# Copies of q and k that write in sequence, pooled scores and local values in other PSUM tiles, and a new order of instructions

## The chip, the cores and the metric
One core of a Trainium2 chip runs the whole kernel in one launch. The metric is device time in microseconds (us). Five engines work on their own instruction lists, each in its list's order: TensorE (PE in the profile, PEld its weight loads), VectorE (DVE), ScalarE (ACT), GpSimd (POOL) and SyncE (SP). SP and ACT also issue the DMAs.

## The reference
Everything is fp32. 2304 tokens (4 batches of 576) pass through an attention and two products with gates:

```python
# attention: per batch and head, S = 576, D = 64, factor 4; scale = 1 / sqrt(D)
q_d, k_d, v_d = means of q, k, v over 4 tokens each
out_up    = repeat(softmax(scale * q_d @ k_d.T) @ v_d, 4)
out_local = softmax(where(|i - j| < 4, scale * q @ k.T, -1e9)) @ v
x = (out_up + out_local)                 # as (2304, 512)
# first layer: d_ff = 2048
h = x @ w_in;  x = (h * sigmoid(1.702 * h)) @ w_out
# second layer: d_ff = 1024
out = ((x @ w1) * (x @ w2) @ w3) @ w_out2
```

## The kernel before
**Products.** Each fp32 product is made of three (`mm3`, lines 305 to 307): both operands are split into a high and a low part by `split` (a copy on ScalarE, line 301, and a subtraction, line 302, mostly on VectorE), and the four 128-row pieces of the inner dimension add up in one PSUM bank. The weights come in as 64-bit numbers, read as pairs of 32-bit words; ScalarE (line 353) and three operations on VectorE (lines 360 to 366) make fp32 of them.

**Stages.** From the start to about 110 us TensorE makes the product of w3 and w_out2 (`w34_transpose`, `w34_mm`), and the attention of batch 0 is woven in between. Then come the first layer's five blocks of up to 512 tokens: for each of 16 slices f of the hidden width an `h_step` (4 x 3 products into a bank, gelu `g_t` on ScalarE at line 810, split) and, two slices later, a `y_step` (into four banks y0 to y3). The attention of batches 1 to 3 is woven into these until about 405 us. Then the second layer runs, with seven half-size products in the place of eight (`ab_step`), to the end.

**Attention.** The heads go in 16 pairs, n = 4 b + hp, two heads on the 128 partitions. Of a pair, `t_piece` transposes q and k on TensorE (line 471, four transpositions into one tile) and ScalarE copies the tile out (line 472): in PSUM the elements stand as (r, u), with r the place within a group of four tokens and u the group; in SBUF as (u, r). That is so in batches 0 and 1, 4 copies a pair, 32 in all; in batches 2 and 3 VectorE transposes. `s_local` makes local scores in two halves (line 515), bounds them by the mask (518) and takes the maximum (519). `s_pool` makes the pooled scores (`ps_sp`, products on line 534) and their maximum (536). In batches 0, 2 and 3 the exponentials read the pooled scores out of PSUM piece by piece (`s_exp`, line 495, `own_exp` True); in batch 1 VectorE subtracts the maximum first and one exponential follows. `p_piece` transposes the weights of the softmax (577) and copies them out (578). `v_pool` makes pooled values (`ps_vp`, products on line 592) and copies them out with a factor (`od`, line 595). `v_local` makes local values in two halves (line 604, 10 and 8 products), adds the pooled ones (608, reads the PSUM tile and `od`) and stores the sum to x_d (612). In the four pairs of `LOCAL` (12 to 15) the local part is not on TensorE but on VectorE and GpSimd, and only pooled scores and values go through PSUM.

**PSUM.** There are eight banks: y0 to y3 (pool `psy`, one tile each; products of w3 and w_out2, then second products of the first layer), two of tag "h" (pool `psh`: first products of the first layer and transposed w3, line 759) and two of tag "t" (pool `pst`: all PSUM tiles of attention). A tile of a tag gets its bank when the tile before the last of that tag has been read by all that read it.

**What sets the order.** `ORDER` (lines 20 to 185) has for each engine a list of positions in the program's own sequence ("12+7" are 12 to 19), and `ACROSS` (186 to 205) pairs of positions on two engines, such as "2:18<4:21". At the end of the program both are put in as dependences without a semaphore, so the scheduler must keep that order. Weights, windows of v (`att_load_v`) and all stores go out on SP, most loads of q, k and v on ACT until batch 2; POOL makes the masks (`setup`). Other tags touched: "ys", "g" and "xr" in SBUF (pool `g2p`, two tiles each); "ys" holds the local results `xo`, the products `w34s` and others, "xr" the tiles of x loaded for the first layer, "g" gelu's output.

Of the kernel before, what the change touches and what calls it, by code (L numbers as in the profile page):

```python
# [8 lines left out]
F32 = mybir.dt.float32  # L9
# [199 lines left out]
def fused_kernel(ctx, tc, q, k, v, w_in, w_out1, w1, w2, w3, w_out2, out):  # L209
# [313 lines left out]
    def s_pool(n, own_exp):  # L523
# [3 lines left out]
        if not near:  # L527
            s_tiles(n, own_exp)
        kd, ep = at["kd", n], at["ep", n]
        ps = pst.tile([128, NPB, SD], F32, tag="t", name="ps_sp")  # L530
        for j in range(NPB):
            for h in range(2):
                p = slice(h * D, (h + 1) * D)
# [660 lines left out]
```

## Time and profile before
| | |
|---|---|
| median of 3 runs | 848.36 us (846.52 to 849.78) |
| the profiled execution | 847.67 us |
| its span in the profile | 845.8 us |
| mean granted TensorE clock | 0.998 |
| busy: PE, PEld, DVE, ACT, POOL | 826.1, 709.1, 581.8, 393.5, 109.2 us |

The span runs from the first to the last recorded work; the execution's own time is 1.9 us longer. Busy times are sums over the span, so one engine's 98% says that it had at most 2% of holes, not where these are. PE and PEld are the same engine's products and weight loads; they overlap.

### The profile page before, as it was taken

To read this page: it belongs to the slowest core of one execution; us is meant where nothing else is said; L and a number is where in the kernel's file an instruction comes from. 1 tells how busy PE (TensorE), PEld (TensorE's weight loads), DVE (VectorE), ACT (ScalarE), POOL (GpSimd) and SP (SyncE) were. 2 spreads that over 40 slices of the span, in tenths; PEclk is the share of its full clock that TensorE was granted. 3 is DMA by queue.
4 is the path that set the end of the run, shared out by engine and by line. 5 is a ranking of instruction groups with operands and counts; after the bars stand their busy time and mean duration, and the time that the engine had idled before them with its cause. 6 is when DMAs were issued, how large, how long until landed. Compare 5 with 4: busy or idle time off the path is not lost.

```text
span 845.8 us, 13672 instructions
## 1 busy us (share of the span) xinstructions
PE 826.1 (98%) x5132; PEld 709.1 (84%) x5132; DVE 581.8 (69%) x1069; ACT 393.5 (47%) x852; POOL 109.2 (13%) x105
## 2 busy tenths in 40 slices
PE   5899999999999999999999999999999999999998
PEld 4677788788788778888899988889998999899996
DVE  6998899999988978586877743335547445654550
ACT  4777787877565563544665544331113111321110
POOL 5342301121333331230000000000000000000000
PEclk9999999999999999999999999999999999999999
DMA  9878796776734366444686538105556454725422
GB/s 262 258 218 233 213 260 173 215 190 185 160 96 101 95 122 156 111 95 123 225 308 231 202 132 351 72 31 193 204 221 223 142 224 182 264 103 218 176 87 74
DMA packets 140597, 150.75 MB, mean 178 GB/s; under 512 B 86898, under 2 KB 121460, under 8 KB 136436
## 3 DMA queue, kind: packets, MB, share of 16 engines
q1 hardware_dynamic: 119424, 141.21, 52.6%
q10 hardware_dynamic: 21108, 8.69, 4.6%
q8 instruction: 40, 0.66, 0.3%
q14 instruction: 25, 0.20, 0.1%
HBM read 117.75 MB, written 32.11 MB: 177 GB/s over the span
## 4 chain that ended last, share of the span: by engine, by line
PE 93%; DVE 3%; DMA 2%; ACT 1%; SPq 1%; issue 0%; ACTq 0%; DVEq 0%
PE ps_h L305 8%; PE ps_y L305 8%; PE ps_y L307 8%; PE ps_y L306 8%; PE ps_h L307 8%; PE ps_h L306 8%; PE ps_ab L305 7%; PE ps_ab L307 7%; PE ps_ab L306 7%; PE ps_o L306 4%; PE ps_o L307 4%; PE ps_o L305 4%; PE ps_pt L577 2%; PE ps_s L515 2%; PE ps_v L604 2%; PE ps_sp L534 2%
## 5 line engine op out<-in xcount | busy, mean ns | idle before, releaser
L305 PE MATMUL ps_h<-x_t,w 128*128 128x512 f32 (+1 forms) x320 | 116.9, 374 | 0.0
L307 PE MATMUL ps_h<-x_t,w 128*128 128x512 f32 (+1 forms) x320 | 116.7, 371 | 0.0
L306 PE MATMUL ps_h<-x_t,w 128*128 128x512 f32 (+1 forms) x320 | 116.5, 371 | 0.1
L307 PE MATMUL ps_y<-gh,w 128*128 128x512 f32 (+1 forms) x320 | 115.6, 373 | 0.0
L305 PE MATMUL ps_y<-gh,w 128*128 128x512 f32 (+1 forms) x320 | 114.0, 374 | 0.0
L306 PE MATMUL ps_y<-gl,w 128*128 128x512 f32 (+1 forms) x320 | 113.1, 371 | 0.0
L307 PE MATMUL ps_ab<-b_t,a_in 128*128 128x384 f32 x336 | 112.5, 335 | 0.0
L305 PE MATMUL ps_ab<-b_t,a_in 128*128 128x384 f32 x336 | 112.5, 335 | 0.0
L306 PE MATMUL ps_ab<-b_t,a_in 128*128 128x384 f32 x336 | 112.4, 334 | 0.0
L302 DVE TENSOR_TENSOR gl<-g_t,gh 128x512 fp32r<-128x512 f32 (+1 forms) x80 | 53.3, 669 | 48.5 <-ACT gh L301 48.3
L301 ACT ACTIVATE abh<-ab 128x384 fp32r<-128x384 f32 x24 | 12.6, 526 | 137.2 <-DVE ab L935 137.2
L810 ACT ACTIVATE g_t<-ps_h 128x512 f32<-128x512 f32 (+1 forms) x80 | 43.8, 552 | 67.0 <-PE ps_h L307 62.8
L305 PEld LDWEIGHTS ps_h<-x_t,w 128*128 128x128 f32 x320 | 60.0, 188 | 10.9 <-issue 0.8
L306 PEld LDWEIGHTS ps_h<-x_t,w 128*128 128x128 f32 x320 | 60.1, 188 | 10.1 <-DVE x_t L302 0.5
L307 PEld LDWEIGHTS ps_h<-x_t,w 128*128 128x128 f32 x320 | 59.8, 188 | 10.2 <-issue 0.2
L305 PEld LDWEIGHTS ps_y<-gh,w 128*128 128x128 f32 x320 | 59.4, 188 | 10.5 <-ACT gh L301 0.5
L307 PEld LDWEIGHTS ps_y<-gh,w 128*128 128x128 f32 x320 | 59.7, 188 | 10.1 <-issue 0.4
L306 PEld LDWEIGHTS ps_y<-gl,w 128*128 128x128 f32 x320 | 59.5, 188 | 10.1 <-issue 0.4
L305 PEld LDWEIGHTS ps_ab<-b_t,a_in 128*128 128x128 f32 x336 | 63.1, 188 | 0.9
L306 PEld LDWEIGHTS ps_ab<-b_t,a_in 128*128 128x128 f32 x336 | 63.1, 188 | 0.9
L307 PEld LDWEIGHTS ps_ab<-b_t,a_in 128*128 128x128 f32 x336 | 63.0, 188 | 0.0
L301 ACT ACTIVATE gh<-g_t 128x512 fp32r<-128x512 f32 (+1 forms) x80 | 46.7, 587 | 22.5 <-PE ps_y L307 21.1
(146 smaller groups left out, 1612.5 us busy)
## 6 DMA issues: line engine op xcount, KB each, us to landing
a_in<-a_d SPq DMA_DIRECT2D x24, 1792.0 KB
st<-in_moe_w_dram SPq DMA_DIRECT2D x32, 512.0 KB
a_d<-ap SPq DMA_DIRECT2D x8, 1792.0 KB
st<-in_moe_w_out_dram SPq DMA_DIRECT2D x24, 512.0 KB
st<-in_moe_w_in_dram SPq DMA_DIRECT2D x16, 512.0 KB
yr<-y_d SPq DMA_DIRECT2D x12, 384.0 KB
out_dram<-osb SPq DMA_DIRECT2D x17, 256.0 KB
s_v<-in_v_dram ACTq DMA_DIRECT2D x15, 288.0 KB
```

The lines of the kernel that those rows point to most:

```text
L301: nc.scalar.activation(hi, raw, AF.Copy)
L302: lo_eng.tensor_tensor(lo, raw, f32(hi), op=ALU.subtract)
L305: nc.tensor.matmul(ps, ll, rh, start=start, stop=False, skip_group_check=more)
L306: nc.tensor.matmul(ps, lh, rl, start=False, stop=False, skip_group_check=more)
L307: nc.tensor.matmul(ps, lh, rh, start=False, stop=stop, skip_group_check=more)
L515: nc.tensor.matmul(ps[p, i - i0], qT[p, i * QB:(i + 1) * QB], kT[p, w0:w0 + KW], start=True, stop=True)
L534: nc.tensor.matmul(ps[p, j], qd[p, j * PB:j * PB + QB], kd[p], start=True, stop=True)
L577: nc.tensor.transpose(ps[:, i - i0], src, ident)
L604: nc.tensor.matmul(ps[p, (i - i0) * QB:(i - i0 + 1) * QB], vw[:, i - i0, h], at["PT", n, i // NPH][:, i % NPH, h * QB:(h + 1) * QB], start ...
L810: nc.scalar.activation(g[:, :n], ps[:, :n], AF.Gelu_apprx_sigmoid)
```

## The change
- Line 472: the copy reads the PSUM tile as (u, r) and writes SBUF in sequence; before, it read PSUM in sequence and wrote every fourth element.
- `s_pool`: the pooled scores of the 12 pairs outside `LOCAL` take a tile of pool `psh`, tag "h", which they share with first products and transposed w3.
- `v_pool` and `v_local`: for these 12 pairs the pooled values' tile is 320 columns wider, and the first half of the local values goes into its rest. It took a tile of its own before.
- `w34_mm`: the first half's four tiles `w34s` take tags "g" and "xr" in turn; the second half's stay with "ys".
- `ORDER` and `ACROSS` are new for all five engines. The program's own sequence of instructions is the same, so the positions mean the same instructions.

```diff
@@ -19,190 +19,190 @@
 ORDER = {
     "PE": (
-        "4+7 0+3 12+7 28 37+1 40+2 57+7 43+6 39 68+5 34+1 20+3 36 29+4 65 74+2 66 77+2 54+1 84 67 85 80 24 81 "
-        "25+2 56 86+1 50+1 82 99 106 92 107 95 52+1 96 93+1 83 113+1 108 97+1 115 124+1 100+1 131 126 132 102+3 "
...
+        "4+6 0 11 1+2 12 16+3 13+2 28+1 37+1 40 57+7 41+4 34 46+3 35+1 39 20+3 31+1 30 33 74+2 65 54+1 77 66 78 "
+        "56 79 24+2 84 27 67 80 85+2 81 50 68+5 99 92 51+2 82 93+1 83 113 95+1 102 114 103+2 115 150 124+1 100 "
...
     "DVE": (
-        "0 2 4 1 3 5 7+1 6 10 12 9 11 14 33 23 13 16 36 34 24 26 37 25 15 35 17 28 19 30 21 18 27 20 29 31 22 49 "
-        "40 38+1 41 32 51 42 50 44 43 46 52 62 45 53 63 54 65 64 56 47 67 48 55 76 75 78 69 84 66 70 77 85 59 68 "
...
+        "0 2 4 1 3 5 8 6 10 7 12 9 11 14 33 16 13 23 34 24 18 35 25 15 26 17 28 19 27 21 20 29 31 22 30 36+1 49 "
...
     "Activation": (
-        "0+1 4 6+1 5 16 10 2 11 17 12 19 3 18 8 14 13 9 35 34 36 26 23 37 22 15 31+1 24 20+1 38 29 39 33 25 30 40 "
...
+        "0+1 4+1 7 16 6 2 11 10 12 17 3 18+1 8 14 13 32 22 9 34 24 15 26 20+1 38 31 39 25 29 23 35 33 36+1 30 27 "
...
     "Pool": (
-        "2 0+1 8 17 11 21 9 28 18 29 19+1 10 15+1 12+2 22+2 26 25 27 30+1 3 34 6 32+1 35+1 39+1 37+1 43 41 44 42 "
...
+        "0+1 8 21 28 19 29 20 13+1 2 11 17+1 9+1 15+1 12 3 22+2 26 25 27 30+1 34 32+1 35+1 39+1 37+1 43+1 41+1 47 "
...
     "SP": (
-        "0+1 8 2+1 6 4+1 7 9 17 10 18 21 19 11 20 22 15 23+2 16 14 12 26+1 13 37 36 38 28 34 52+1 30 29 31 43 39 "
...
+        "0+2 8 3 5+1 4 7 9 17 10 18 21 19+1 22 15 14 23+1 16 12 25 11 26+1 13 36+2 52 34 28 30 29 31 53 43 33 "
...
 ACROSS = (
-    "0:2202<1:778 0:2980<1:779 0:3028<1:792 0:3460<1:876 0:3466<1:875 0:3940<1:972 0:3946<1:971 1:74<2:96 "
...
+    "0:2202<1:778 0:2980<1:779 0:3028<1:792 0:3460<1:876 0:3466<1:875 0:3940<1:972 0:3946<1:971 1:146<2:160 "
...
@@ -469,7 +469,7 @@
             ps = pst.tile([128, FAC, UC], F32, tag="t", name="ps_t")
             for r in range(FAC):
                 nc.tensor.transpose(ps[:, r], st[:, c, r].rearrange("p h d -> p (h d)"), ident[:UC, :UC])
-            nc.scalar.activation(dst[:, c * UC:(c + 1) * UC].rearrange("p u r -> p r u"), ps, AF.Copy)
+            nc.scalar.activation(dst[:, c * UC:(c + 1) * UC], ps.rearrange("p r u -> p u r"), AF.Copy)
...
@@ -527,7 +527,7 @@
         if not near:
             s_tiles(n, own_exp)
         kd, ep = at["kd", n], at["ep", n]
-        ps = pst.tile([128, NPB, SD], F32, tag="t", name="ps_sp")
+        ps = (psh if near else pst).tile([128, NPB, SD], F32, tag="h" if near else "t", name="ps_sp")
...
 
     def v_pool(n):
         PT, vd = at["PT", n, 1], at["vd", n]
-        ps = pst.tile([128, SD], F32, tag="t", name="ps_vp")
+        both = at["psv", n] = pst.tile([128, SD + (0 if n in LOCAL else HQ * QB)], F32, tag="t", name="ps_vp")
+        ps = both[:, :SD]
         for kc in range(2):
...
@@ -597,7 +598,10 @@
     def v_local(n, i0, i1):
         vw, od = at["vw", n, i0 // HQ], at["od", n]
         xo = g2p.tile([128, NB], F32, tag="ys", name="xo")[:, :(i1 - i0) * QB]
-        ps = pst.tile([128, (i1 - i0) * QB], F32, tag="t", name="ps_v")
+        if i0 == 0:
+            ps = at["psv", n][:, SD:]
+        else:
+            ps = pst.tile([128, (i1 - i0) * QB], F32, tag="t", name="ps_v")
         for i in range(i0, i1):
...
@@ -768,7 +772,7 @@
                 acc34[i] = psy.tile([128, NB], F32, tag=f"y{i}", name="ps_w34")
             mm3(acc34[i], t[:, 0, i], t[:, 1, i], wo[:, 0], wo[:, 1], j == 0, j == NF2 - 1)
             if j == NF2 - 1:
-                sb = g2p.tile([128, NB], F32, tag="ys", name="w34s")
+                sb = g2p.tile([128, NB], F32, tag="ys" if half else "g" if i % 2 else "xr", name="w34s")
                 nc.scalar.activation(sb, acc34.pop(i), AF.Copy)
                 nc.sync.dma_start(out=w34_d[:, half * 4 + i, :], in_=sb)
             pump()
```

## Rows read from the trace of the kernel before

**Rows 1.** The profile's page, its first part: busy us, share, instructions.

```profile
span 845.8 us, 13672 instructions
...
PE 826.1 (98%) x5132; PEld 709.1 (84%) x5132; DVE 581.8 (69%) x1069; ACT 393.5 (47%) x852; POOL 109.2 (13%) x105
```

**Rows 2.** Stretches: from:to, length, busy PE, PEld, DVE, ACT, POOL, clock, DMA, GB/s.

```profile
20.00:40.00 20.00, 17.40 (x97) 13.04 (x95) 19.80 (x39) 14.75 (x44) 5.91 (x4) 0.91 0.88 253
80.00:100.00 20.00, 18.97 (x171) 14.52 (x169) 17.37 (x33) 14.71 (x45) 5.65 (x6) 1.00 0.78 199
120.00:200.00 80.00, 79.93 (x586) 64.61 (x585) 77.37 (x140) 61.61 (x103) 13.31 (x11) 1.00 0.71 196
```

**Rows 3.** Chain of waits that ended last: start us, us, what.

```profile
75.92 5.36 DMA x_d<-xo
...
489.21 0.47 PE ps_h L306 x2
```

**Rows 4.** TensorE's waits: us in all, times, longest us.

```profile
PE ps_t L471 <- DMA s_q<-in_q_dram: 8.9, 1, 8.9
...
PE ps_t L471 <- DMA s_k<-in_k_dram: 1.0, 1, 1.0
```

**Rows 5.** Timeline, 25 to 38 us: start, us, instruction, [idle before, releaser].

```profile
28.00 0.41 PE L759 MATMUL ps_w<-ident,dec 128*128 128x128 f32 x2 [1.77 <-DVE dec L366]
...
37.57 0.11 PEld L577 LDWEIGHTS ps_pt<-ident,el 128*72 128x72 f32 x1 [0.84 <-ACT PT L578]
```

**Rows 6.** Timeline of weight loads, 67 to 94 us.

```profile
71.31 0.55 PEld L604 LDWEIGHTS ps_v<-PT,vw 72*64 72x64 f32 x16 [0.79 <-DVE xo L608]
...
91.62 0.48 PEld L604 LDWEIGHTS ps_v<-PT,vw 72*64 72x64 f32 x12 [1.28 <-ACT ep L495]
...
93.39 0.55 PEld L604 LDWEIGHTS ps_v<-PT,vw 72*64 72x64 f32 x16 [0.45 <-ACT od L595]
```

**Rows 7.** ScalarE's groups: xcount, busy us, mean ns, idle before.

```profile
L578 ACT ACTIVATE PT<-ps_pt 72x512 f32<-72x512 f32 x36 | 20.6, 592 | 17.6 <-PE ps_pt L577 17.3
...
L472 ACT ACTIVATE qT<-ps_t 128x288 f32<-128x288 f32 x16 | 10.8, 688 | 5.3 <-PE ps_t L471 5.3
...
L578 ACT ACTIVATE PT<-ps_pt 72x384 f32<-72x384 f32 x20 | 9.5, 484 | 12.6 <-PE ps_pt L577 12.5
```

**Rows 8.** VectorE's groups, 200 to 420 us.

```profile
L653 DVE TENSOR_REDUCE r<-s 128x9 f32<-128x63 f32 x4 | 1.1, 264 | 1.2 <-ACT el L495 1.0
...
L652 DVE TENSOR_TENSOR s<-s,near 128x63 f32<-128x63 f32 x4 | 0.8, 210 | 0.5 <-DVE s L647 0.5
```

**Rows 9.** Waits of TensorE's weight loads, whole run.

```profile
PEld ps_s L515 <- issue: 2.8, 8, 0.4
PEld ps_vp L592 <- issue: 2.4, 9, 0.4
...
PEld ps_s L515 <- ACT kT L472: 0.7, 1, 0.7
```

**Rows 10.** Timeline of the end.

```profile
841.78 0.38 ACT L958 ACTIVATE osb<-ps_o 128x256 f32<-128x256 f32 x1 [10.28 <-PE ps_o L307]
...
842.20 0.42 DVE L960 COPY osb<-ps_o 128x256 f32<-128x256 f32 x1 [5.21 <-ACT osb L958]
```

**Rows 11.** Timeline, 254 to 265 us.

```profile
255.25 0.71 PE L592 MATMUL ps_vp<-PT,vd 72*64 72x144 f32 x8
...
256.01 0.29 ACT L595 ACTIVATE od<-ps_vp 128x144 f32<-128x144 f32 x1 [2.85 <-PE ps_vp L592]
...
258.04 0.60 ACT L810 ACTIVATE g_t<-ps_h 128x512 f32<-128x512 f32 x1 [1.74 <-PE ps_h L307]
...
264.38 0.38 ACT L495 ACTIVATE ep<-ps_sp,nb 128x144 f32<-128x144 f32 x1
```

**Rows 12.** Timeline, 65 to 74.5 us.

```profile
65.24 0.54 SPq L341 DMA_DIRECT2D st<-in_moe_w_dram  x1
...
73.97 0.42 DVE L360 TENSOR_SCALAR st<-st 128x512 int32<-128x512 int32 x1
```

341 rows, old and new, of tables (ACROSS, ORDER) are left out of this document.

## The prediction, before the change was run

> **What bounds the kernel now.** I read the busy shares first, then stretches of time, then who waits for whom, then single places of the timeline. TensorE is busy 826.1 of 845.8 us; VectorE, at 581.8 us, is far behind over the whole [rows 1]. That average hides stages. From 20 to 40 us TensorE has only 17.40 us of work while VectorE has 19.80, and the granted clock is 0.91; from 80 to 100 us TensorE has 18.97 us; from 120 to 200 us it is full (79.93 of 80) and VectorE nearly so (77.37) [rows 2]. Later one 512-column product follows the other every 0.23 us [rows 3]. The lists of order differ up to position 2734 of 4540 on TensorE, which is work that starts before 486 us; the 360 us behind it are untouched, and from about 405 us no attention is left. So what can be won lies in the first 405 us, and as TensorE is full from 120 us on, most of it in the first 120 us, in holes of TensorE: the first operands' landing (8.9 us, then 1.0 us for k) [rows 4], a hole of 1.77 us before 28.00 us that VectorE's decoding ends, 0.84 us before a transposition of weights of the softmax, 0.79 us and 1.28 us before value products [rows 5, 6].
>
> **The change part by part.** The sum is made against the profiled execution, 847.67 us (span 845.8 and 1.9 outside it); the median of the runs, 848.36 us, is 0.7 above it, so this execution is a typical one.
>
> *Copies of q and k (line 472).* 32 copies stay 32 copies; only the strides change sides. Now q's take 688 ns each (k's some more). The same engine copying out of PSUM in sequence takes 592 ns for 512 columns and 484 for 384, 0.84 ns a column [rows 7]; on that line 288 columns cost 0.40 us. That is the low end. For the other end a strided read has to be priced, and the nearest row is VectorE's reduction over 63 elements read with a stride, 264 ns, where its minimum over the same 63 in sequence takes 210 ns [rows 8]; 54 ns over 63 elements is 0.86 ns an element, which brings the copy to 0.40 + 288 x 0.86 = 0.65 us, nearly what it is now. I take the low end, since its rows are the same engine out of the same memory. ScalarE then has 32 x 0.29 = 9.3 us less to do, but it is busy for 61.61 of 80 us in the densest of these stretches [rows 2], so only copies that TensorE waits for count. The profile names one, 0.7 us before the first local scores [rows 9]; there two copies follow k's landing: -0.3 us, from 0 to -0.6. The cover of the others is the products of w3 and w_out; if it is gone each costs 0.29 us.
>
> [...]
>
> *Pooled scores in the pool of the first products, pooled and local values in one tile.* No instruction is added. Each of the 12 head pairs outside LOCAL now takes two tiles fewer from the pool of two banks with tag t. What goes: the 1.28 us before 91.62, where value products wait for the exponentials that read pooled scores, and the 0.79 us before 71.31, where the second half of a pair's values waits for the first half's addition [rows 6]. In the first five pairs the new order puts the second half, which has its own bank, before or into the first. Next in line at both places is product work that is ready, so I book 1.28 + 0.79 = -2.1 us whole; if a bank is still missing there, zero.
>
> *What this adds: a wait.* The copy of the pooled values (line 595) reads the tile into which the first local values are now written. That two engines don't share a tile's bank is seen at the end of the kernel: VectorE waits 5.21 us for ScalarE's copy of the other half of the same accumulator, though it needs nothing of it [rows 10]. So TensorE must wait for that copy. The price is in the rows twice: pooled values end at 255.25 + 0.71 = 255.96 and the copy runs from 256.01 to 256.30, 0.34 us behind them [rows 11]; the wait for such a copy that ends at 93.39 is 0.45 us [rows 6]. I take 0.40. In the new list of TensorE the first local values stand directly behind the pooled ones in 6 of the 12 pairs (positions 947, 1123, 1433, 1576, 1709 and 1832), and in two more only a few products lie between. Queued behind on TensorE is everything, as it works in order. 6 x 0.40 + 2 x 0.2 = +2.8 us; zero if no such wait is made, and with one more operation of ScalarE (0.60 us, such as g_t) ahead of each copy 8 x 1.0 = +8 [rows 11].
>
> *Order sought anew.* TensorE's positions move by at most 67 places, all other engines' by at most 20. Going from wide products to the 64-column ones costs some 0.35 us of weight loading (2.8 us in 8, 2.4 in 9) [rows 9]. I counted the changes between the two kinds in both lists: 28 become 32 up to position 560, and 56 become 50 behind it, one entry fewer in all: -0.3 us. The 0.84 us before 37.57 is filled in the new list with single products of w3 and w_out between the transpositions: -0.8, or zero if those products wait as well. The hole before 28.00 stays: in the new list of VectorE the decode that ends it moves ahead of another decode and of the pooled maximum, but the pooled products move behind the hole as well, so TensorE arrives earlier by as much. q's first load goes out ahead of v's; TensorE then waits for k as before [rows 4], so zero. Late next after all this is VectorE, 17.37 of 20 us busy between 80 and 100 us [rows 2]: it can take up the 2.1 us, hardly more. On POOL and SP setup masks, loads of v and the stores of w34 change places; the first four tiles of w34s now come from the tags g and xr, so xo is not held up by them, but the first load of x_d into a tile of xr waits for such a store on SP, with a load of w3 and windows of v behind it. That load is issued at 65.24 us and first used by VectorE at 73.97 [rows 12], 8.7 us of cover, more than the 5.36 us that the slowest store in the chain of waits took to land [rows 3]; if the cover is gone, VectorE loses the rest. Zero.
>
> Sum: -0.3 - 2.1 + 2.8 - 0.3 - 0.8 = -0.7 us, 847.0 us; the order's own hits and misses at places that I can't follow I bound by the holes that are left, about 3 us either way.
>
> **The rivals.**
> *The hole before 28 us closes.* Then its 1.77 us go, and with it the loss of clock in that stretch: the granted clock of 0.91 over 20 us is 1.8 us [rows 2], and TensorE had been idle just before. For it: the decode is earlier on VectorE by two operations. Against: VectorE is busy 19.80 of 20 us there. 847.0 - 3.6 = 843.4 us.
> *Slower: a bank of the first products is held.* The pooled scores now sit in one of only two banks with tag h until the third exponential has read them: in the profile from about 255.2 (their last product) to 264.38 + 0.38, 9.6 us [rows 11]. In that time the first products of some two blocks of f have one bank, so each must wait until g_t has read the one before, 0.60 us [rows 11], unless second products stand between. For it: the exponentials queue behind g_t, gh and local exponentials on ScalarE. Against: the list mixes first and second products, and three second products (3 x 0.23) already cover the 0.60. It decides where fewer than three stand between. 8 pairs x 2 steps x 0.6 = +9.6 us on the forecast: 856.6 us.
> *The change doesn't do what it says:* strided reads cost what strided writes did and the freed banks were not what TensorE waited for. Then only the added wait is left: 847.7 + 2.8 = 850.5 us.
>
> **How the numbers follow.** Some 0.5% (4.2 us) is what a measurement of this kernel can tell from no change: below 844.1 is faster, above 852.6 slower. The forecast (847.0 with 3 either way) has 0.45; with the hole closed 0.30; nothing but the wait 0.12; the held bank 0.13. The closed hole is faster nearly always (0.27 of its 0.30), and 0.03 of the forecast falls there too: 0.30. The held bank gives 0.13 slower, and the wait at its upper bound 0.03: 0.16. The rest, 0.54, is within. The range around 847.0 goes from 840.5 (the hole closed, 843.4, and 3 us of other holes) to 852.5 (the forecast with the wait at its upper bound of 8 us); the likeliest case alone has 844 to 850.
>
> **What would show it.** Copies of 288 columns at 0.40 us, or still at 0.69, settle the first term. Waits of TensorE's weight loading for od of 0.4 us at six places settle the third; none there means that the added wait costs nothing. Waits for ep exponentials and xo before value products should be gone. A wait of first products for ep or mx speaks for the held bank. If the granted clock between 20 and 40 us reads 1.00 and the hole before 28 us is gone, the faster rival holds. The forecast is wrong if the time from 490 us to the end, 356 us long, differs by over 0.5 us, or if TensorE's holes in the first 110 us shrink by more than 5 us.

## The result: 0.6% slower

The changed kernel takes 853.37 us (median of 7 runs, 852.10 to 856.38), the kernel before 848.35 (7 runs beside it): 5.0 us more, ratio 1.0063 with a 95% interval of 1.0042 to 1.0084. The forecast was 847.0, the range ended at 852.5. The execution in its profile took 856.38 us (span 854.5 and 1.9 outside), 3.0 us above its own median, so its trace has to be read with that in mind. First the page's first part, to be held against [rows 1]:

```profile
span 854.5 us, 13683 instructions
...
PE 829.9 (97%) x5132; PEld 711.3 (83%) x5132; DVE 579.0 (68%) x1069; ACT 389.3 (46%) x854; POOL 111.8 (13%) x105
```

TensorE's busy time grew by 3.8 us, the span by 8.7: more than half of the loss is new idle time. The stretches of [rows 2], and three more (columns: stretch, length, busy PE, PEld, DVE, ACT, POOL, granted clock, DMA share, GB/s):

```profile
20.00:40.00 20.00, 17.52 (x118) 13.16 (x116) 18.49 (x39) 14.64 (x45) 5.62 (x4) 1.00 0.84 251
80.00:100.00 20.00, 18.65 (x175) 14.31 (x173) 17.29 (x33) 13.59 (x42) 4.59 (x4) 1.00 0.85 209
120.00:140.00 20.00, 18.07 (x95) 13.98 (x94) 15.51 (x29) 13.79 (x24) 4.85 (x4) 0.91 0.71 208
120.00:200.00 80.00, 77.69 (x556) 61.98 (x557) 71.97 (x131) 56.81 (x100) 15.01 (x13) 0.98 0.64 186
200.00:340.00 140.00, 137.09 (x1018) 110.48 (x1015) 122.50 (x213) 78.89 (x195) 43.03 (x34) 1.00 0.54 125
499.00:849.00 350.00, 350.00 (x1777) 319.16 (x1777) 168.87 (x317) 85.87 (x168) 0.00 (x0) 1.00 0.46 171
```

In the kernel before, the stretch from 200 to 340 us was:

```profile
200.00:340.00 140.00, 139.77 (x1014) 112.10 (x1013) 122.35 (x216) 78.10 (x194) 42.81 (x34) 1.00 0.55 127
```

From 20 to 40 us there is no loss of clock this time. The busy times there, 17.52 and 17.40 us, do not compare as work, since at 0.91 the same products are busy for longer (a 128x512 product of lines 305 to 307 takes 459 ns in the mean there, 438 in the changed kernel). From 120 to 200 us, where TensorE had been full with 79.93, it has 77.69, and from 200 to 340 us it lacks 2.9 of 140 us, where it lacked 0.2. The last 350 us are full, as before. So most of the loss lies where no hole was. Who ends these holes, by the waits of weight loads and of products in the whole run (us in all, times, longest):

```profile
PEld ps_vp L608 <- ACT od L596: 6.1, 11, 0.9
PE ps_vp L608 <- ACT od L596: 3.3, 9, 0.7
```

Eleven waits for the copy of pooled values, `od`, 6.1 us of weight loading in all (four of them before 140 us, 1.6 us together). In [rows 6] there was one, of 0.45 us. One of them in full (timeline: start, us, instruction, [idle before, releaser]):

```profile
174.19 0.44 PEld L593 LDWEIGHTS ps_vp<-PT,vd 72*64 72x64 f32 x8
174.19 0.71 PE L593 MATMUL ps_vp<-PT,vd 72*64 72x144 f32 x8
174.95 0.29 ACT L596 ACTIVATE od<-ps_vp 128x144 f32<-128x144 f32 x1 [2.32 <-PE ps_vp L593]
...
175.29 0.66 PEld L608 LDWEIGHTS ps_vp<-PT,vw 72*64 72x64 f32 x20 [0.66 <-ACT od L596]
175.29 0.80 PE L608 MATMUL ps_vp<-PT,vw 72*64 72x64 f32 x20 [0.39 <-ACT od L596]
```

The last pooled product ends at 174.90, the copy runs to 175.24, and only at 175.29 does the first weight of the local values load: the loader is idle for 0.66 us (from 174.63, where the pooled loads end), since it would have run on under the pooled products and now can't (run 2 shows it running on, at 169.75 us). TensorE's products have a gap of 0.39 us at the same place.

The second large hole of this execution is one that the text of the forecast did not name:

```profile
127.45 0.47 PE L471 MATMUL ps_t<-ident,s_q 72*128 72x72 f32 x4 [1.93 <-DMA s_q<-in_q_dram]
```

TensorE waits for a half of q, whose load stands 8 places later in ScalarE's new list (issued at 119.60 us). Behind it the granted clock is 0.91 over 20 us, 1.8 us. Whether that hole belongs to the change or to this execution is asked of the first, the fourth and the seventh run below.

The copies of q and k, against [rows 7]:

```profile
L472 ACT ACTIVATE qT<-ps_t 128x288 f32<-128x288 f32 x16 | 6.3, 406 | 6.6 <-PE ps_t L471 5.4 <-issue 1.1
L472 ACT ACTIVATE kT<-ps_t 128x288 f32<-128x288 f32 x16 | 6.1, 403 | 3.8 <-PE ps_t L471 3.7
```

0.41 us for 0.69: the low end of the forecast's bounds.

### The profile page after: what moved, and what is told of

It reads as the page before. It is cut to its first block, busy times and chain, and to the rows that moved or that the text cites. A ratio compares the mean times of both kernels' runs of the same rounds, so it can differ in the third digit from the quotient of the medians.

```text
span 854.5 us, 13683 instructions
## 1 busy us (share of the span) xinstructions
PE 829.9 (97%) x5132; PEld 711.3 (83%) x5132; DVE 579.0 (68%) x1069; ACT 389.3 (46%) x854; POOL 111.8 (13%) x105
## 4 chain that ended last, share of the span: by engine, by line
PE 87%; DVE 4%; DMA 4%; ACT 2%; issue 1%; SPq 0%; ACTq 0%; POOL 0%; DVEq 0%; POOLq 0%
PE ps_y L305 8%; PE ps_y L307 7%; PE ps_y L306 7%; PE ps_h L305 7%; PE ps_h L307 7%; PE ps_h L306 7%; PE ps_ab L307 7%; PE ps_ab L305 7%; PE ps_ab L306 7%; PE ps_o L306 4%; PE ps_o L307 4%; PE ps_o L305 4%; PE ps_pt L577 2%; DMA st<-in_moe_w_in_dram 2%; PE ps_s L515 2%; DMA s_q<-in_q_dram 2%
## 5 line engine op out<-in xcount | busy, mean ns | idle before, releaser
L366 DVE SCALAR_TENSOR_TENSOR dec<-dec,st 128x512 int32<-128x512 int32 x72 | 52.8, 739 | 5.4 <-ACT dec L353 4.2
```

The lines of the kernel that those rows point to most:

```text
L366: nc.vector.scalar_tensor_tensor(t, t, 3, st[:, :, 0], op0=ALU.logical_shift_left, op1=ALU.bitwise_or)
```

## The experiments

There were fifteen further runs; a ratio is always to the kernel before on the same chip. **Theory A:** the wait that the shared tile makes is the loss, and the other edits together give about nothing. **Theory B:** the new order loses at other places (a later load of q, the first 30 us), and the wait only takes what another would. **Theory C** came up on the way: time won at the start is taken up by what is late next there, VectorE with the weights. Where a run's own text gives A and B another meaning, that one counts for the run.

**1. The changed kernel again** (no edit).

> The changed kernel once more, unaltered, for its spread and for a second profile. Its profile showed TensorE idle for 1.93 us at 127 us until a load of q had landed, then a granted clock of 0.95 and 0.88 for 20 us (1.7 us lost), in an execution of 856.4 us, 3.0 above the kernel's median of 853.4. Theory A (the hole at 127 us is luck of that execution): this profile shows no such hole, or one under 0.5 us, with a time of 852 to 854. Theory B (the hole belongs to the new order, since the load is issued 8 places later on ScalarE): it is there again, over 1.5 us. In both theories the waits of first local values for the copy of the pooled ones come back, 8 to 9 of them, 0.4 to 0.7 us each.

852.87 us (6 runs, 851.17 to 856.43), ratio 1.0059 [1.0040, 1.0078]. Its profiled execution was once more its slowest, 856.43 us, yet there is no hole at 127 us. It has another one earlier (timeline, then stretches as above):

```profile
97.70 0.30 PE L577 MATMUL ps_pt<-ident,el 128*72 128x128 f32 x1 [1.89 <-ACT PT L578]
```

```profile
100.00:120.00 20.00, 19.77 (x146) 16.12 (x143) 14.44 (x27) 11.82 (x23) 2.29 (x3) 0.78 0.68 202
120.00:140.00 20.00, 19.75 (x110) 15.80 (x109) 19.34 (x34) 16.54 (x29) 5.06 (x4) 1.00 0.83 227
```

The granted clock is 0.78 over the 20 us behind that hole, 4.4 us lost. So in both profiles a hole of 1.9 us and the clock behind it are more than what the execution lies above its median (3.7 against 3.0 us, 6.3 against 3.6), at another place each time. As far as this run goes the wait for q is chance (theory A), but run 7 has it again. The waits for `od` come back at the same eleven places, 5.7 us in all.

**2. The copy reads from elsewhere.** Nothing reads pooled values, so nothing must wait for the copy.

```diff
-        nc.scalar.activation(od, ps, AF.Copy, scale=1.0 / FAC)
+        nc.scalar.activation(od.rearrange("p (a b) -> p a b", a=2) if n not in LOCAL else od,
+                             ident[:, :UC].unsqueeze(1).to_broadcast([128, 2, UC]) if n not in LOCAL else ps,
+                             AF.Copy, scale=1.0 / FAC)
```

> The changed kernel, but in the 12 head pairs outside LOCAL the copy that makes od (line 596) reads a constant in SBUF in the place of the pooled values' PSUM tile, so pooled values are left out of the result and nothing has to wait for that copy before it writes to the tile. All orders stay. Theory A (the added wait makes the kernel slower): the 8 to 9 waits of 0.4 to 0.7 us are gone, 5 to 6 us less than the changed kernel: 847.5 to 849, no slower than the kernel before. Theory B (the new order loses elsewhere, the wait only takes what another would): 851 to 853.5.

848.29 us (11 runs), ratio 0.9994 [0.9983, 1.0006]: 4.6 us less than the first run by the medians, 5.5 by the ratios. The same place as above in its trace:

```profile
169.33 0.44 PEld L593 LDWEIGHTS ps_vp<-PT,vd 72*64 72x64 f32 x8
169.34 0.71 PE L593 MATMUL ps_vp<-PT,vd 72*64 72x144 f32 x8
169.75 0.73 PEld L608 LDWEIGHTS ps_vp<-PT,vw 72*64 72x64 f32 x20
169.88 0.75 PE L608 MATMUL ps_vp<-PT,vw 72*64 72x64 f32 x20
```

The local values' first weight loads at 169.75, while the pooled products run. Theory A as expected, B is out. It also shows the other half of the answer: without the wait all other edits and the new order together change the time by -0.06% (-0.17% to +0.06%), some -0.5 us, where -3.5 us had been booked. No run separates the moved pooled scores, the tags of `w34s` and the order from each other.

**3. Products between pooled and local values.** Three wide products move ahead at six places, here the first.

```diff
-946+3 956+9 990 932+1 952
+946+3 990 932+1 956+9 952
```

> The changed kernel with one edit in TensorE's order: at the six places where the first local values stand directly behind the pooled ones, three 512-column products (3 x 0.23 us) that stood behind them go in between. Theory A (the wait for the copy costs 0.67 us at each of six places): the products cover it, but each place has one more change from wide to narrow products, some 0.35 us, so 6 x (0.67 - 0.35) = 1.9 us less than the changed kernel, 851.5; with the change of kind free, 4 us less, 849.4. Theory B (the waits are not what costs): no faster than the changed kernel, up to 2 us slower by the added changes of kind, 853 to 855.5.

851.72 us, ratio 1.0039 [1.0025, 1.0054], about 1.1 to 2.0 us under the changed kernel, which is where theory A has it with the price of a change between wide and narrow products paid at each place; but the interval overlaps the first run's, so by itself this gain is likely and not shown. The waits of weight loads that it left, and the loads that nothing released (2 of these, 0.7 us, in the changed kernel):

```profile
PEld ps_vp L612 <- ACT od L600: 3.9, 6, 2.3
PEld ps_vp L612 <- issue: 2.5, 7, 0.4
```

The 11 waits for `od` became 6, one of them 2.3 us long and none of the others over 0.5, and five changes of kind came in at 0.36 us each.

**4. The load of q back at its old place** in ScalarE's list.

```diff
-188 187 184 192 162 190 198 163 197
+197 188 187 184 192 162 190 198 163
```

> The changed kernel with one edit in ScalarE's order: the second load of q of the pair that TensorE waited for at 127 us goes 8 places forward, where it stood before the change. Theory A (that wait is luck of the profiled execution): within 0.7 us of the changed kernel. Theory B (the later issue costs in most executions, the wait and the loss of clock behind it): 2 to 3.5 us less, 850 to 851.5, and in the profile no wait for q near 127 us.

852.86 us, ratio 1.0050 [1.0035, 1.0064]: no difference to the first run. Theory A; the later load is not where the median's time went.

**5. Local values later, without a further change of kind.** At the first of six places:

```diff
-946+3 956+9 990 932+1 952 943+1 953 966 954+1 967+4 980+5 945 1010 972+7
+946+3 990 932+1 952 943+1 953 966 954+1 967+4 980+5 945 1010 956+9 972+7
```

> The changed kernel, whole, with one edit in TensorE's order: at the six places where first local values stand directly behind the pooled ones, these first local values go further back, into or behind the narrow products that stand next in the list (the second local values, or the rest of the first), so that no change between wide and narrow products is added. Theory A (the wait for the copy is what made the kernel slower, 4.7 us of it by the run that took it away): four of the six waits go and at two some 0.25 us is left, 6 x 0.67 - 2 x 0.25 = 3.5 us less than the changed kernel, 849.5. Theory B (a later addition and a later free bank cost what the wait gives back): no faster than 852.

851.75 us, ratio 1.0039 [1.0026, 1.0052]: a miss for the 849.5 of theory A, though the waits themselves went:

```profile
PEld ps_vp L611 <- ACT od L599: 1.9, 6, 0.5
```

4.2 us of waiting for `od` are gone and only 1.1 to 2.0 us came out, and its interval too overlaps the first run's. In this profile TensorE waits instead for the additions that follow the moved products (0.7, 0.5 and 0.2 us for `xo`) and for `gl` (1.1 us at three places, 0.4 at one in the changed kernel). These are 2.1 us, as theory B's mechanism, a later addition, would have it; that they are what took the rest back is read from one profile and not tested. Moving the values is not a remedy.

**6. Copies in sequence alone**, in the kernel before.

```diff
-dst[:, c * UC:(c + 1) * UC].rearrange("p u r -> p r u"), ps, AF.Copy)
+dst[:, c * UC:(c + 1) * UC], ps.rearrange("p r u -> p u r"), AF.Copy)
```

> The kernel before with one edit: the 32 copies of q and k read PSUM strided and write in sequence, as in the changed kernel, whose copies took 0.40 us where they took 0.69 to 0.71. Theory A (the forecast's term: ScalarE is seldom waited for): 0.3 us less than before, no difference that can be measured. Theory B (each copy stands on the way to the scores in the first 110 us, 16 of the 32 copies by 0.29 us): 2 to 4 us less, 845.

847.85 us, ratio 0.9988 [0.9976, 1.0000]: 1.0 us less, between 0 and 2, so nearer to the forecast's term than to theory B's. Its median is the lowest of all whole kernels here, but its interval reaches 1.0000, so it is not shown to be faster than the one before.

**7. Old copies in the changed kernel** (the reverse edit).

> The changed kernel with the copies of q and k as before, 0.29 us longer each, all else as changed. Theory A: within 1 us of the changed kernel. Theory B (the new order leans on the shorter copies, since it was made with them): 2 to 4 us more, 855 to 857.

853.44 us, ratio 1.0052 [1.0037, 1.0068]: no difference to the changed kernel. There the copies are worth nothing that can be measured. Its profiled execution, 856.64 us and once more the slowest, has the hole of the first profile again, with a clock of 0.91 from 120 to 140 us:

```profile
127.74 0.47 PE L471 MATMUL ps_t<-ident,s_q 72*128 72x72 f32 x4 [2.06 <-DMA s_q<-in_q_dram]
```

So the wait for q is not chance alone. With the later load it comes in some executions (1.93 and 2.06 us here, 1.12 in run 2, 0.2 in run 1); by run 4 the median does not show it.

**8. The kernel before with the copy from elsewhere** (edit of run 2).

> The kernel before with the edit of the second run: od is copied from a constant in SBUF, so pooled values are left out of the result. It shows what that edit gives by itself, where local values have a tile of their own and wait for the copy at one place (0.45 us). Theory A (the edit's gain in the changed kernel was the added wait): 0 to 1 us less than before. Theory B (the edit gains since additions and free banks come earlier, whatever the tiles): 3 to 5 us less, 844 to 846.

848.80 us, ratio 0.9992 [0.9977, 1.0006]. Taking the read away gives nothing where the tiles are separate. So what run 2 won is the shared tile's wait, and not an earlier `od`.

**9. The first nine loads as before**, in the changed kernel.

```diff
-"0+2 8 3 5+1 4 7 9
+"0+1 8 2+1 6 4+1 7 9
```

> The changed kernel with one edit in SP's order: its first nine loads stand as in the kernel before (v, then both halves of q, weights, then both halves of k). In the changed kernel the first half of q lands at 7.2 us, but TensorE then waits 1.8 us for the second half and 1.7 us for k, and starts the first wide product at 14.1 us where it did at 13.5 before. Theory A (these loads are where the new order loses at the start): the first wide product starts at 13.5 us and the kernel is 0.6 to 1 us faster, 852. Theory B (what follows takes it up, as decoded weights are late next): no difference, 852.9 to 853.4.

853.68 us, ratio 1.0068 [1.0043, 1.0092]: no gain. The first wide product didn't start at 13.5 us but at 14.69, since q landed later (9.23 us) and ScalarE's copies of q held up k. So what was taken for a loss at the start didn't come back, and is not shown to be one.

**10 and 11. q and k first**: run 5's kernel and run 6's kernel with SP's list beginning "0 1 2 3 4 5 6 7 8" (0, 1, 6 and 7 are weights, 2 and 3 q, 4 and 5 k, 8 v).

> The fifth run's kernel (local values later in TensorE's order) with q and k loaded straight behind the first two weights on SP, ahead of the next weights and of v. Theory A (q's and k's landing sets TensorE's start): q lands at some 8 us and k at some 9.5, 3 us earlier; the first wide products start 2 us earlier, and 1 to 2 us of it are left at the end: 850 to 850.8. Theory B (VectorE's decoding sets the first 100 us): the hole moves to the products of w3, no difference to the fifth run, 851.7.

> The kernel before with the sequential copies of q and k and the same early loads of q and k; order else as before, no PSUM tile moved. Theory A: 1 to 2 us less than the sixth run (847.9), 846 to 847, the first version that beats both kernels. Theory B: the same as the sixth run, 847.5 to 848.3.

856.73 us, ratio 1.0094 [1.0073, 1.0115], and 852.32, ratio 1.0047 [1.0032, 1.0062]: both some 4 to 5 us slower than without the edit, which neither theory had. In run 11 q lands early, at 6.7 us, and the price comes 13 us later (timelines of GpSimd, VectorE and TensorE in turn, and a stretch):

```profile
13.67 1.37 POOL L483 TENSOR_TENSOR s_v<-s_v 72x512 f32<-72x512 f32 x1 [4.12 <-DMA s_v<-in_v_dram]
```

```profile
19.30 0.90 DVE L519 TENSOR_TENSOR el<-ps_s,band 128x288 f32<-128x288 f32 x2 [2.47 <-POOL band L293]
```

```profile
19.81 1.04 PE L535 MATMUL ps_sp<-kd,qd 64*64 64x144 f32 x12 [3.00 <-DVE el L519]
```

```profile
20.00:40.00 20.00, 17.65 (x91) 13.88 (x88) 18.84 (x38) 12.82 (x41) 5.91 (x5) 0.83 0.74 218
```

The edit had put v behind the weights; GpSimd waits 4.12 us for it with the last masks (`band`) queued behind, VectorE waits 2.47 us for the masks, TensorE 3.00 us for VectorE, and behind that the clock is 0.83 over 20 us, 3.4 us where the kernel before lost 1.8 [rows 2]. (This profile is of the fastest execution of run 11, 849.77 us.) Run 10 shows the same chain: 5.16 us for v, 4.35 us for the masks, and TensorE 3.18 us for a decode. The displaced v was the edit's own fault and no answer to its question, so it was put again:

**14 and 15. q and k early, v kept ahead of the weights**: run 6's kernel with "0 1 8 2 3 4 5 6 7" and with "0 1 2 3 8 4 5 6 7".

> The sixth run's kernel with SP's list beginning 0 1 8 2 3 4 5 6 7: v stays ahead of q as before, and only the one load of weights that stood between q and k goes behind k. Theory A (v's displacement made runs 10 and 11 slow, and k's landing counts): no wait for v on GpSimd, TensorE no longer waits for k, 0.4 to 1 us less than the sixth run, 846.9 to 847.5. Theory C (VectorE takes up what TensorE wins at the start, or the weights' later landing does): as the sixth run, 847.5 to 848.5. If it is 852 as run 11, displaced weights were the cause there and not v.

> The sixth run's kernel with SP's list beginning 0 1 2 3 8 4 5 6 7: q ahead of v, v ahead of k, weights behind. q lands about 1 us earlier than in the run with v first. Theory A: another 0.5 to 1 us less, 846 to 847. Theory C: as the sixth run, 847.5 to 848.5, since the decoded weights are next. GpSimd should not wait for v by more than some 1 us in either theory.

848.96 us, ratio 1.0002 [0.9987, 1.0017], and 848.04, ratio 0.9996 [0.9980, 1.0011]: level with the kernel before, and 0.2 to 1.2 us above run 6, on which they are built. Run 14 differs from run 11 in v's place alone, so v's displacement was the cause there; run 10, which has the same waits, was not put again. In both TensorE no longer waits for k, and in run 15 it starts at 6.78 us; then it stands before the first product of w3 and w_out2, in run 14 and in run 15:

```profile
14.44 1.22 PE L306 MATMUL ps_w<-w,w3t 128*128 128x512 f32 x2 [2.36 <-DVE w3t L762]
```

```profile
13.34 1.22 PE L306 MATMUL ps_w<-w,w3t 128*128 128x512 f32 x2 [1.49 <-DVE w3t L762]
```

It waits for the low part of w3, which VectorE makes; in run 6 no such wait was longer than 0.7 us. That is theory C. What is won at the start is waited for a few us on.

**12. The shared tile alone, where values stand directly behind.** Kernel before, its order untouched.

```diff
-        ps = pst.tile([128, SD], F32, tag="t", name="ps_vp")
+        both = at["psv", n] = pst.tile([128, SD + (HQ * QB if n in (0, 3, 6, 7, 11) else 0)], F32, tag="t", name="ps_vp")
+        ps = both[:, :SD]
...
-        ps = pst.tile([128, (i1 - i0) * QB], F32, tag="t", name="ps_v")
+        if i0 == 0 and n in (0, 3, 6, 7, 11):
+            ps = at["psv", n][:, SD:]
+        else:
+            ps = pst.tile([128, (i1 - i0) * QB], F32, tag="t", name="ps_v")
```

> The kernel before, its order untouched, with only the shared tile for pooled and first local values, and only in the five pairs (0, 3, 6, 7 and 11) in which local values stand directly behind pooled ones in TensorE's order. Theory A (each place of this kind costs a wait of 0.6 to 0.7 us for the copy of the pooled values): 5 x 0.67 = 3.3 us more than before, 851.9, with waits for od in the profile at five places more than the one of before. Theory B (the changed kernel lost by its order, and the shared tile costs nothing by itself): no difference, 848.0 to 849.

850.29 us, ratio 1.0027 [1.0013, 1.0042]: 2.3 us more (1.1 to 3.6) for five places. Waits of weight loads and of products, and one place in the timeline:

```profile
PEld ps_vp L608 <- ACT od L596: 3.4, 5, 0.7
PE ps_vp L608 <- ACT od L596: 2.0, 5, 0.5
```

```profile
201.71 0.66 PEld L608 LDWEIGHTS ps_vp<-PT,vw 72*64 72x64 f32 x20 [0.66 <-ACT od L596]
```

Five waits, 0.66 to 0.72 us of the weight loader each, at the five pairs; the one of [rows 6], at a tile of its own, is there as before. The mechanism is shown alone, in an order that was made without it. The measured price lies between TensorE's gaps, 2.0 us, and the loader's idle time, 3.4 us.

**13. The shared tile where values stand apart**, pairs 1, 4, 5, 8, 9 and 10, on run 6's kernel (edit as in run 12 with these pairs).

> The sixth run's kernel (order before, copies in sequence) with the shared tile in the other six pairs (1, 4, 5, 8, 9 and 10), where 8 to 43 wide products stand between pooled and first local values. Theory A: no wait for od, since the products between take 1.8 us and more; and pair 1 gets a bank more, so the 0.79 us in which its second half of values waited for the first half's addition goes: 847.0, faster than before. Theory B (any sharing costs, since the tile is held until the addition): 1 us and more above the sixth run, 849 or more. Theory C (the bank's gain is taken up by what is late next): 847.8.

848.79 us, ratio 1.0014 [0.9998, 1.0030], against 0.9988 for run 6. There is one wait for `od` at a shared tile, of 0.6 us, so at five of six places with products between, the wait is gone, as theory A says. But the gain of the freed bank isn't there: the wait of a second half of values for an addition, 0.79 us in [rows 6], stands at 71 us as it did. That the kernel came out above run 6 rather than level with it (theory B or C) is not explained by its waits, and stays open.

## Why the prediction was wrong

**The first failed step is the price of the added wait.** The forecast saw the wait, inferred it from a like one at the end of the kernel [rows 10], and named the six places; it booked 0.40 us each and 0.2 at two more, +2.8 us. The wait measured 4.6 to 5.5 us (run 2); in the trace the weight loader is idle for 0.66 to 0.93 us at the six places. Two things were mis-sized. The 0.40 lay between the time from the pooled products' end to the copy's end (0.34 us [rows 11]) and a wait of the weight loader that was partly covered (0.45 us [rows 6]); where nothing stands between, the loader is idle for 0.66 us, since without the wait it loads the next group's first weight under the last products (run 2, 169.75 us). The kernel's price lay between the products' gaps (3.3 us in sum) and the loader's idle time (6.1 us). And the waits are 11, not 8: some of batch 0 wait too, where second values stand in between but don't cover it.

The wait is there although the two use different columns of the tile: local values in columns of their own wait until the copy of the pooled ones has ended, 175.24 and then 175.29 us. What would come of both at once no run here shows.

**The second failed step, the larger one: "I book 1.28 + 0.79 = -2.1 us whole", and the order's own hits and misses put at nothing, with 3 us either way.** In the changed kernel no value product waits for `ep` or for the first half's `xo` any more, as forecast. But run 2, in which the added wait is gone, is no faster than before, so the 2.1 us, the 1.1 of the order and the 0.3 of the copies, 3.5 in all, came to some 0.5 us (1.4 by one end of the interval, a loss of 0.5 by the other). The waits of TensorE's products in the changed kernel's first 110 us show others in their place:

```profile
PE ps_t L471 <- DMA s_q<-in_q_dram: 8.9, 2, 7.2
PE ps_t L471 <- DMA s_k<-in_k_dram: 1.7, 1, 1.7
PE ps_w L305 <- DVE w3t L765: 1.3, 2, 0.8
PE ps_pt L577 <- ACT PT L578: 1.0, 1, 1.0
```

q is as late in sum as in [rows 4], k 0.7 us later, and there are waits for the low part of w3 and for a bank of transposed softmax weights. Still the start was won, and lost again behind it. Stretches of run 2's profile, then of the kernel before (from 140 to 200 us both are full, but for 0.07 us):

```profile
0.00:100.00 100.00, 85.87 (x742) 66.88 (x743) 85.78 (x163) 68.88 (x197) 40.42 (x48) 1.00 0.86 244
100.00:120.00 20.00, 19.43 (x130) 14.98 (x130) 18.69 (x34) 15.30 (x29) 0.99 (x1) 1.00 0.87 242
120.00:140.00 20.00, 18.88 (x101) 14.69 (x102) 17.75 (x33) 15.20 (x27) 4.88 (x4) 1.00 0.72 196
200.00:340.00 140.00, 138.93 (x1011) 113.01 (x1008) 126.39 (x218) 78.23 (x195) 42.91 (x34) 1.00 0.53 126
```

```profile
0.00:100.00 100.00, 84.68 (x691) 65.88 (x691) 84.65 (x159) 70.35 (x193) 37.09 (x47) 0.98 0.85 237
100.00:120.00 20.00, 20.00 (x172) 16.41 (x172) 19.27 (x33) 15.48 (x28) 3.36 (x3) 1.00 0.91 264
```

In the first 100 us TensorE has 14.1 us of holes in the place of 15.3, and loses no clock where the kernel before lost 1.8 us [rows 2]: 3.0 us won. From 100 to 340 us it has 2.8 us of holes where the kernel before has 0.3: 2.5 us lost, most of it behind 120 us, where the forecast took TensorE to be full. The longest are for the later load of q (1.12 us at 124 us) and for `gl`, the low part of gelu, which VectorE makes (0.53 us at 113 us, 0.48 at 222). These are single executions (spans 846.0 and 845.8 us), so the sums hold to about 1 us. The forecast named VectorE as late next, with 2.1 us to take up, and gave it no price. Runs 14 and 15 show that it has one at the start; here it is a part of what was lost, and the new order's load of q another.

**Copies:** right in size (0.40 us; the term of -0.3 lies within 0 to -2 in run 6, and run 7 shows no difference). The other end, 0.65 us, which the forecast worked out from VectorE's strided reduction [rows 8], did not come: ScalarE's copies took 0.41.

**The hole before 28 us** was to stay. In the changed kernel's profile its longest wait for a decode is 0.6 us, and from 20 to 40 us no clock is lost; but holes of 1.9 us with a loss of clock of their own appeared at 127 and at 97 us in its two profiles. That rival came true at its place: its clock is in the 3.0 us that the start won, and went with them.

**The held bank:** no first product waits for `ep` or `mx` in the changed kernel's waits; this rival is out. **The end:** the last 350 us are full in both, as forecast.

By the sum: -0.3 - 2.1 + 2.8 - 0.3 - 0.8 = -0.7 was forecast, about -0.5 + 5 was measured, +5.0 by the medians. Of the 5.7 us between, some 3 are gains that did not last and some 2 to 3 the wait's price. The upper bound that the forecast gave to the wait (+8) held it, but that bound had 0.03 of the chance; the loader's idle time, from the end of the pooled weights to the end of the copy, could have been read from the same place of the timeline as [rows 11]. With 5 us for the wait and nothing booked as won, the sum is 853 us, "slower".

## What to carry to other kernels

Where two engines come to share a PSUM tile, count a full drain for each place where the second use stands directly behind the first: end of the products, the copy, and the weight load that can no longer run ahead (0.66 to 0.93 us of the loader at the six places here, 0.66 to 0.72 at five in run 12); look in the order for these places before anything else. Two sums bounded the price of these waits: the gaps between products (3.3 us in the changed kernel, 2.0 in run 12) and the weight loader's idle time (6.1 and 3.4); measured were 4.6 to 5.5 and 2.3 us. And a new order is to be read beyond the stage that it wins: here 3.0 us were won in the first 100 us, and 2.5 were lost behind them, where TensorE had been full.

## What the runs showed that was not expected

- A strided read of PSUM by ScalarE (288 columns, steps of 288 bytes) is as quick as one in sequence (0.84 ns a column from [rows 7] is 0.24 us for 288, and 0.40 with the fixed part): 0.41 us, where the same copy with a strided write to SBUF took 0.69.
- The clock's price behind a hole can exceed the hole: 1.89 us of idle TensorE at 97 us, then 0.78 over 20 us, 4.4 us; but 1.93 us at 127 us, then 0.91 over 20 us, 1.8 us. Such a clock is a mean over its stretch: in run 1 the 128x512 products start every 0.43 us from 106.81 to 108.09 us and every 0.23 us from 109.22 to 110.38 us. The same hole can have a price or none: the 1.77 us before a transposition of w3 stand in the kernel before (at 28.00 us, 0.91 from 20 to 40 us) and in run 15 (at 27.20 us, a mean clock of 1.000 over the whole span).
- One load of 288 KB put back by six places in SP's list cost 4 to 5 us of 848, by way of GpSimd's order (run 11 against runs 6, 14 and 15).
